# Sinkhorn's sums by products, the last pair's forms made at first use, and eight staging rows: one change to a three-layer kernel

## The chip, the core and the metric

The kernel runs on one core of a Trainium2 chip. The metric is the device time of one execution in microseconds (us). A core has five engines that run side by side and wait for one another by semaphores: TensorE (PE), VectorE (DVE), ScalarE (ACT), GpSimd (POOL) and SyncE (SP), which here issues all transfers; each works through its instructions in one fixed order.

## The reference

Linear attention on 4 x 8 heads, then a dense layer pair, then eight experts on 2304 tokens, each expert weighted by a gate that is normalised by rows and columns eight times:

```python
logits = x @ w_gate                       # 2304 x 8
P = np.exp(logits - logits.max())
for _ in range(8):
    P /= P.sum(1, keepdims=True) + 1e-09
    P /= P.sum(0, keepdims=True) + 1e-09
    P *= N / E
for e in range(E):                        # w1[e]: 512 x 1024, w2[e]: 1024 x 512
    out += P[:, e:e + 1] * (np.maximum(x @ w1[e], 0.0) @ w2[e])
```

## The kernel before

The first 650 us hold the attention part and the dense layers. The change concerns the experts after them. Their work is a list `order` of 48 positions (p, q): eight experts in two halves of their hidden width are p, and q counts three pairs of token blocks (2 x 384 tokens each). A position n has a layer 1 and a layer 2. Each is a 2x2 block product with seven products instead of eight (Winograd's scheme); the seven stand in `SLOTS` as p1, p5, p6, p3, p7, p2, p4. A product (L828) is twelve instructions of 128x384, since every operand is split into a high and a low part and three of the four part products are kept.

The left operands are "forms" of the weights (`split_forms`, seven for each layer, made on POOL, ACT and DVE), the right operands forms of the tokens: b11, t1, t2, b22, t3, b21, t4, where b are the blocks and t their differences. `split_form` makes one: a cast on ACT (L604) and a subtraction on DVE (L605). The token forms of a pair are made once, stored to DRAM as `xv`, and loaded for each expert half into one of four buffers `xvv` (768 KB a form, L700), the next one when a slot's product has freed a buffer. Pairs 0 and 1 are made during the last dense layer; for pair 2, `forms(NPR - 1, ...)` makes them beside layer 1 of position 0 (differences on POOL, L629) and sums the gate logits with twenty 128x384 products (L636) and transposes (L648).

Layer 1 leaves four hidden blocks r; `hidden_forms` makes their seven forms (differences on POOL, L852). In the main loop layer 2 of position n and layer 1 of position n + 1 alternate slot by slot, and `tick()` takes one step of a side task each time: first `sinkhorn`, then `gate_first`, which multiplies the accumulated first expert by its gate (L965), at the end `finish_pair`, which transposes (L977), copies (L978) and stores rows. Experts from the second on have the gate multiplied into their hidden blocks (L892), and so need the gate table `prT` in DRAM.

`sinkhorn` sums columns over partitions by an all-reduce on POOL, nine times. The program is reordered by a scheduler, so that the code's order and the engines' orders differ.

Of the kernel before, what the change touches and what calls it, by code (L numbers as in the profile page):

```python
# [20 lines left out]
def tile_features_attention__moe__sinkhorn_moe(  # L21
# [578 lines left out]
    xv = dram.tile([NPR, NS, P, 2 * KH * NB], F32, name="xv")  # L600
    prT = dram.tile([NE, (NTT + 3) // 4 * 4 * P], F32, name="prT")
# [5 lines left out]
    def forms(q, temp, part_, pg, turned, eng):  # L607

        t0 = 2 * NB * q

        def b(k, j):
            return accT[:, KH * (k - 1) : KH * k, t0 + (j - 1) * NB : t0 + j * NB]


        uses = {"b21": [(0, 1)], "t1": [(1, 0)], "b11": [(0, 0), (1, 0)], "b22": [(1, 1)]}
        done = [0, 0]
        of = {}
        for nm in ("b21", "t1", "b11", "b22", "t2", "t4", "t3"):
            if nm[0] == "b":
                src = b(int(nm[1]), int(nm[2]))  # L620
            else:
# [7 lines left out]
                eng.tensor_sub(src, lhs, rhs)  # L629
            v = part_()  # L630
            split_form(src, v)
            nc.sync.dma_start(xv[q, FORMS.index(nm)], v.bitcast(F32).rearrange("p a k n -> p (a k n)"))
            for blk, k in uses.get(nm, ()):
# [8 lines left out]
        for blk in range(2):  # L642
            gs = temp("gs").rearrange("p k n -> p (k n)")[: 2 * NE, :NB]
            nc.scalar.copy(gs, pg[blk][: 2 * NE, :NB])
            pt = turned()
# [3 lines left out]
            i0 = t0 // P + blk * nt  # L649
            nc.scalar.copy(lt[:, i0 : i0 + nt], pt[:, :nt])  # L650
            yield

    def early_forms(q, pool):
        return forms(
            q,
            lambda nm: pool.tile([P, KH, NB], F32, tag="t", bufs=2, name=nm),
            lambda: pool.tile([P, 2, KH, NB], F32R, tag="v", bufs=3, name="xvs"),
            [psm.tile([P, 512], F32, tag="sm", name="psg") for _ in range(2)],
            lambda: psm.tile([P, 4, 2 * NE], F32, tag="sm", name="pt"),
            nc.vector,  # L660
        )
# [55 lines left out]
    for p in range(1, N1):  # L717
# [10 lines left out]
        for bi, (t0, n) in enumerate(blocks):  # L728
# [17 lines left out]
            if last and bi % 2 and bi < len(blocks) - 1:  # L746
                side.append(early_forms(bi // 2, xs))
# [24 lines left out]
    def allred(out, in_, op):  # L772
        nc.gpsimd.partition_all_reduce(out, in_, P, op)

    def sinkhorn():
        nc.vector.tensor_add(pr, lt[:, :, 0:NE], lt[:, :, NE : 2 * NE])
        mx = mb.tile([P, 1], F32, name="mx")
        nc.vector.tensor_reduce(mx, pr, AX.XY, ALU.max)
        mg = mb.tile([P, 1], F32, name="mg")
        allred(mg, mx, bass_isa.ReduceOp.max)  # L780
        yield
# [3 lines left out]
        for _ in range(8):  # L785
# [6 lines left out]
            nc.vector.tensor_reduce(cs, pr.rearrange("p t e -> p e t"), AX.X, ALU.add)  # L792
# [189 lines left out]
    def fetch_both(p):  # L982
        for _ in fetch(p):
            pass
# [90 lines left out]
```

## Time and profile before

| | |
|---|---|
| median of three runs | 2167.4 us (2164.7 to 2167.79) |
| the profiled execution, its own time | 2163.17 us |
| its span, first to last instruction | 2161.4 us |
| busy share PE / DVE / ACT / POOL | 96% / 80% / 40% / 36% |
| mean granted clock of PE | 0.981 |

Times in the rows count from the span's start. A line number such as L828 is that of the kernel before. Only where PE waits or runs at a lower granted clock can a change of the other engines' work gain anything.

### The profile page before, as it was taken

What the parts mean: (1) busy time and instruction counts of PE and PEld (TensorE: products, weight loads), DVE (VectorE), ACT (ScalarE), POOL (GpSimd) and SP (SyncE); (2) the same over time, 40 slices, a digit from 0 to 9 for tenths busy, and PEclk for the clock granted to TensorE, in tenths of its full rate; (3) what the DMA queues carried; (4) which work ended last, traced back from release to release, by engine and by line L of the source; (5) the groups of instructions that cost most, each with busy time, mean ns of one, the idle gap of its engine ahead of it and who ended that gap; (6) DMA issues with size and microseconds to landing.
All of it is one profiled execution on the core that took longest, in us unless ns stands there. A gap on an engine that the chain in (4) does not pass through costs nothing.

```text
span 2161.4 us, 31712 instructions
## 1 busy us (share of the span) xinstructions
PE 2070.0 (96%) x12326; PEld 1930.2 (89%) x12326; DVE 1725.5 (80%) x2167; ACT 872.9 (40%) x1508; POOL 780.0 (36%) x435
## 2 busy tenths in 40 slices
PE   8999999999996749999999999999999999999997
PEld 5566689888996749999999999999999999999997
DVE  5898657585666547999889888998898998988986
ACT  6786643222334315433334333333343333433432
POOL 3443200010005123545435445453354444534431
PEclk9999999999998879999999999999999999999998
DMA  4444241110247326566666666666766666667652
GB/s 117 108 105 116 78 127 57 39 59 1 112 161 287 122 74 240 209 232 210 235 237 225 222 243 223 225 213 228 241 224 223 231 231 229 217 224 244 205 197 96
DMA packets 156325, 381.91 MB, mean 177 GB/s; under 512 B 73616, under 2 KB 79888, under 8 KB 156176
## 3 DMA queue, kind: packets, MB, share of 16 engines
q1 hardware_dynamic: 156176, 379.88, 52.7%
q8 instruction: 99, 1.62, 0.3%
q14 instruction: 50, 0.41, 0.1%
HBM read 354.76 MB, written 24.93 MB: 176 GB/s over the span
## 4 chain that ended last, share of the span: by engine, by line
PE 84%; DVE 7%; DMA 4%; issue 3%; ACT 1%; POOL 1%; SPq 1%; DVEq 0%; POOLq 0%; ACTq 0%
PE psa L828 31%; PE psb L828 30%; PE ps L241 6%; PE ps L242 6%; PE ps L243 6%; DMA rb<-rden 2%; PE kvp L350 1%; PE psn L406 1%; DVE acc L965 1%; PE zp L357 1%; DMA rden<-comp 1%; DVE xl L605 1%; PE psd L415 1%; DVE acc L938 0%; DMA xl<-xv 0%
## 5 line engine op out<-in xcount | busy, mean ns | idle before, releaser
L828 PE MATMUL psb<-xl,xh 128*128 128x384 f32 x2400 | 447.3, 336 | 15.4 <-DVE mu L899 14.2
L828 PE MATMUL psa<-xl,xh 128*128 128x384 f32 x2400 | 449.0, 337 | 7.8 <-ACT xl L604 3.2
L828 PEld LDWEIGHTS psb<-xl,xh 128*128 128x128 f32 x2400 | 421.2, 189 | 16.5 <-DVE mu L899 14.6
L828 PEld LDWEIGHTS psa<-xl,xh 128*128 128x128 f32 x2400 | 422.3, 189 | 9.5 <-ACT xl L604 3.6
L852 POOL TENSOR_TENSOR t<-r,r 128x768 f32<-128x768 f32 x96 | 207.4, 2160 | 513.8 <-DVE r L892 462.2
L852 POOL TENSOR_TENSOR t<-r,t 128x768 f32<-128x768 f32 x96 | 233.8, 2435 | 17.3 <-issue 13.6
L828 PE MATMUL psa<-xl,w2v 128*128 128x384 f32 x960 | 182.8, 338 | 9.9 <-DVE xl L605 5.2
L828 PE MATMUL psb<-xl,w2v 128*128 128x384 f32 x960 | 181.7, 336 | 9.2 <-DVE xl L605 9.2
L938 DVE TENSOR_TENSOR acc<-psb,acc 128x768 f32<-128x768 f32 x163 | 154.9, 950 | 42.8 <-PE psb L828 39.0
L938 DVE TENSOR_TENSOR acc<-psa,acc 128x768 f32<-128x768 f32 x161 | 153.0, 950 | 40.9 <-PE psa L828 37.2
L605 DVE TENSOR_TENSOR xl<-t,xl 128x768 fp32r<-128x768 f32 x131 | 179.9, 1373 | 5.8 <-ACT xl L604 5.7
L828 PEld LDWEIGHTS psa<-xl,w2v 128*128 128x128 f32 x960 | 170.3, 191 | 11.0 <-DVE xl L605 5.6
L828 PEld LDWEIGHTS psb<-xl,w2v 128*128 128x128 f32 x960 | 169.0, 189 | 9.5 <-DVE xl L605 9.5
L604 ACT CAST xl<-t 128x768 fp32r<-128x768 f32 x131 | 109.6, 837 | 115.4 <-POOL t L852 48.4
L390 POOL PARTITION_ALL_REDUCE eq<-eq x64 | 90.9, 1466 | 136.8 <-ACT eq L389 136.8
L241 PE MATMUL ps<-xh,w0h 128*128 128x288 f32 (+3 forms) x384 | 130.9, 341 | 3.3 <-ACT r L262 3.1
L605 DVE TENSOR_TENSOR xl<-r,xl 128x768 fp32r<-128x768 f32 x96 | 130.1, 1356 | 1.7 <-ACT xl L604 0.5
L242 PE MATMUL ps<-xl,w0h 128*128 128x288 f32 (+3 forms) x384 | 129.6, 338 | 0.0
L243 PE MATMUL ps<-xh,w0l 128*128 128x288 f32 (+3 forms) x384 | 129.3, 338 | 0.0
L684 POOL TENSOR_TENSOR s<-wf 128x512 f32<-128x512 f32 x32 | 50.9, 1591 | 212.0 <-DVE xh L605 114.1
L242 PE MATMUL ps<-gl,w1h 128*128 128x288 f32 (+3 forms) x384 | 126.6, 336 | 0.0
L243 PE MATMUL ps<-gh,w1l 128*128 128x288 f32 (+3 forms) x384 | 126.2, 337 | 0.0
(199 smaller groups left out, 3761.1 us busy)
## 6 DMA issues: line engine op xcount, KB each, us to landing
xl<-xv SPq DMA_DIRECT2D x336, 768.0 KB
wf<-in_moe_w_dram SPq DMA_DIRECT2D x32, 1024.0 KB
gate<-prT SPq DMA_DIRECT2D x45, 384.0 KB
xv<-xvs SPq DMA_DIRECT2D x14, 768.0 KB
raw<-in_moe_w_in_dram SPq DMA_DIRECT2D x16, 512.0 KB
raw<-in_moe_w_out_dram SPq DMA_DIRECT2D x16, 512.0 KB
qnat<-in_q_dram SPq DMA_DIRECT2D x16, 288.0 KB
rb<-rden SPq DMA_DIRECT2D x32, 144.0 KB
```

Source lines behind the costliest of these rows:

```text
L241: nc.tensor.matmul(ps, ah, bh, start=first, stop=False)
L242: nc.tensor.matmul(ps, ah, bl, start=False, stop=False)
L243: nc.tensor.matmul(ps, al, bh, start=False, stop=last)
L350: nc.tensor.matmul(kvp[h * D : (h + 1) * D, : 2 * NF], t[:r, i, h], e, start=(i == 0), stop=(i == MT))
L357: ins = nc.tensor.matmul(zp[q0 : q0 + 32, : 2 * NF], ones[:r, :32], e, start=(i < 2), stop=(i >= MT - 1))
L390: nc.gpsimd.partition_all_reduce(eq[:, 1], eq[:, 0], P, bass_isa.ReduceOp.absmax)
L604: nc.scalar.copy(v[:, 0], src)
L605: nc.vector.tensor_sub(v[:, 1], src, v[:, 0].bitcast(F32))
L684: nc.gpsimd.tensor_tensor(s1, a(2, 1), a(2, 2), ALU.add)
L828: nc.tensor.matmul(ps[:, x, :NB], w[:, wi, k, cs], b[:, bi, k], start=first and k + i == 0, stop=k == KH - 1 and i == 2, skip_group_check= ...
L852: nc.gpsimd.tensor_tensor(t[nm], x, y, ALU.subtract)
L938: nc.vector.tensor_add(o, ps, o)
```

## The change

1. The column sums of `sinkhorn` are products of a matrix of ones with the sums per partition, into columns 384 to 511 of the PSUM tile that layer 1's chain a uses at that time (`spare`); the maximum goes to DRAM and comes back broadcast to all partitions. `sinkhorn` starts after position 1 instead of before position 0.
2. The forms of pair 2 are made when position 2 first needs them, straight into the buffers `xvv`, and stored from there for later use; the differences are on POOL as before. The logits of this pair are sixty products of 128x16, issued in layer 1 of position 2, into spare columns too.
3. The output rows go through two tiles allocated once, with eight row slots, instead of a new tile of two rows each time.
4. The two weight loads of a half are issued in two positions instead of one.

```diff
+    def last_form(i, x):
+        q = NPR - 1
+        def diff(nm, lhs, rhs):
+            if nm not in late:
+                late[nm] = hp.tile([P, KH, NB], F32, name="late" + nm)
+            nc.gpsimd.tensor_tensor(late[nm], lhs, rhs, ALU.subtract)
+            return late[nm]
...
+        split_form(src, x.rearrange("p (a k n) -> p a k n", a=2, k=KH))
+        nc.sync.dma_start(xv[q, i], x.bitcast(F32))
...
         while nxt[0] < min(n, NS * len(order)):
             m, i = divmod(nxt[0], NS)
-            nc.sync.dma_start(xvv[nxt[0] % XB].bitcast(F32), xv[order[m][1], i])
+            x = xvv[nxt[0] % XB]
+            if m == NPR - 1:
+                last_form(i, x)
+            else:
+                nc.sync.dma_start(x.bitcast(F32), xv[order[m][1], i])
             nxt[0] += 1
...
         nc.vector.tensor_reduce(mx, pr, AX.XY, ALU.max)
+        nc.sync.dma_start(mxd.rearrange("a p -> p a"), mx)
+        mr = hp.tile([P, 2, NB], F32, tag="gate", bufs=2, name="mr")[:, 0, :P]
+        nc.sync.dma_start(mr, mxd.to_broadcast([P, P]))
+        yield
+        yield
         mg = mb.tile([P, 1], F32, name="mg")
-        allred(mg, mx, bass_isa.ReduceOp.max)
-        yield
+        nc.vector.tensor_reduce(mg, mr, AX.X, ALU.max)
...
             nc.vector.tensor_reduce(cs, pr.rearrange("p t e -> p e t"), AX.X, ALU.add)
+            yield
+            ps = spare["tile"][:, 1, NB + it * NE : NB + (it + 1) * NE]
+            with tc.issue_after(spare["first"]):
+                nc.tensor.matmul(ps, ones, cs, start=False, stop=True, skip_group_check=True)
             cr = mb.tile([P, 1, NE], F32, tag="cr", name="cr")
-            allred(cr[:, 0], cs, bass_isa.ReduceOp.add)
-            yield
-            nc.vector.tensor_scalar(cr, cr, 1e-9, None, ALU.add)
+            nc.vector.tensor_scalar(cr[:, 0], ps, 1e-9, None, ALU.add)
...
+    def logits(nm, x):
+        nt = NB // P
+        o = spare["tile"][:, 0, NB : NB + 2 * nt * 2 * NE].rearrange("p (t e) -> p t e", e=2 * NE)
+        with tc.issue_after(spare["first"]):
+            for blk, k in USES.get(nm, ()):
+                n8 = 4 * KH + 2 * KH * blk
+                for kk in range(KH):
+                    for w, part in ((wg1, 0), (wg2, 1)):
+                        done[blk] += 1
+                        for t in range(nt):
+                            nc.tensor.matmul(
+                                o[:, blk * nt + t], x[:, part, kk, t * P : (t + 1) * P], w[:, KH * k + kk, : 2 * NE],
+                                start=False, stop=done[blk] == n8, skip_group_check=True,
+                            )
+        if nm == "b21":
+            i0 = 2 * NB * (NPR - 1) // P
+            nc.scalar.copy(lt[:, i0 : i0 + 2 * nt], o)
...
+    def finish_rows(t):
+        if not turned:
+            turned.extend(stage(NP, w) for w in range(2))
+        ps = bank("ab"[t // 2 % 2] + "1")
+        for h in range(2):
+            o = turned[t // 4 % 2][:, (t + h) % 4]
...
     for i in range(NS):
         next(l1)
-        next(last)
         next(w2n)
...
-    side.append(sinkhorn())
...
+        if n + 1 == NPR - 1:
+            side.append(sinkhorn())
```

The order of POOL's instructions, from the start of position 0's hidden forms. `mg` and `cr` are all-reduced, `t` are differences of hidden blocks, `s` and `wf` belong to the weight forms, `late` to the last pair's forms; an ISA row without operands is an instruction that the all-reduce brings with it. Before:

```order
L773 ISA
L773 ISA mg<-mx 128x1 [waits DVE_49]
L852 ISA
L852 TENSOR_TENSOR t_7279<-r_7185,r_7234 128x768 [waits Activation_49,Pool_49]
L852 TENSOR_TENSOR t_7283<-r_7211,t_7279 128x768 [waits PE_49,Pool_49]
L852 TENSOR_TENSOR t_7287<-r_7211,r_7185 128x768
L773 ISA
L773 ISA cr<-cs 128x8 [waits DVE_49]
L852 ISA
L852 TENSOR_TENSOR t_7329<-r_7256,t_7283 128x768 [waits Activation_49,Pool_49]
```

After:

```order
L683 TENSOR_TENSOR s<-wf_5_7227 128x512 [waits DMAHW5_49,DVE_49,Pool_49]
L689 TENSOR_TENSOR s<-wf_4_6214,s 128x512 [waits DVE_49]
L685 TENSOR_TENSOR wf_5_7227<-wf_5_7227 128x2x256 [waits Pool_49]
L684 TENSOR_TENSOR s<-s,wf_5_7227 128x512 [waits DVE_49]
L894 TENSOR_TENSOR t_7215<-r_7157,r_7194 128x768 [waits Activation_49]
L894 TENSOR_TENSOR t_7219<-r_7176,t_7215 128x768 [waits Pool_49]
L894 TENSOR_TENSOR t_7223<-r_7176,r_7157 128x768
L894 TENSOR_TENSOR t_7263<-r_7211,t_7219 128x768 [waits Activation_49,Pool_49]
L715 TENSOR_TENSOR latex<-acc,latex 128x768 [waits DVE_49] x2
```

The all-reduces and the instructions that come with them are gone, and the last pair's differences have moved in between the hidden ones.

The order of PE's instructions at the end of position 3 and the start of position 4, the same place by the number of products ahead of it (psa and psb with a number are single PSUM tiles). Before:

```order
L828 MATMUL psa_8164<-xl_88,w2v3_7081 128x384 [waits DVE_49,Activation_49]
L828 MATMUL psa_8164<-xl_88,w2v3_7081 128x384 x11
L828 MATMUL psa_8146<-xl_88,xh_87 128x384 [waits DMAHW0_49,DVE_49]
L828 MATMUL psa_8146<-xl_88,xh_87 128x384 x11
L828 MATMUL psb_8163<-xl_88,w2v4_7082 128x384 [waits DVE_49,Activation_49]
L828 MATMUL psb_8163<-xl_88,w2v4_7082 128x384 x11
L828 MATMUL psb_8371<-xl_88,xh_87 128x384 [waits DMAHW1_49,DVE_49]
L828 MATMUL psb_8371<-xl_88,xh_87 128x384 x11
```

After:

```order
L832 MATMUL psa_8065<-cs_8179,ones_98 128x8 [waits DVE_49,Activation_49]
L867 MATMUL psb_8066<-xl_88,xh_87 128x384 [waits DMAHW0_49,DVE_49]
L867 MATMUL psb_8066<-xl_88,xh_87 128x384 x11
L867 MATMUL psa_8065<-xl_88,xh_87 128x384 [waits DMAHW7_49,DVE_49]
L867 MATMUL psa_8065<-xl_88,xh_87 128x384 x11
L867 MATMUL psb_8338<-xl_88,xh_87 128x384 [waits DMAHW1_49,DVE_49]
L867 MATMUL psb_8338<-xl_88,xh_87 128x384 x11
L832 MATMUL psa_8065<-cs_8252,ones_98 128x8 [waits DVE_49]
L867 MATMUL psa_8065<-xl_88,xh_87 128x384 [waits DMAHW2_49,DVE_49]
L867 MATMUL psa_8065<-xl_88,xh_87 128x384 x11
```

The ones products (L832) wait for DVE's column sums in the middle of PE's queue, and the layer-1 product after the second one writes to the same tile and waits for DVE; layer 2's products have moved away from here.

The order of SP's transfers where the gate table `prT` is stored. Before:

```order
L812 DMA prT<-tp 40x1x32 [waits DMAHW6_49]
L812 DMA prT<-tp 40x1x32 [waits DMAHW7_49]
L812 DMA prT<-tp 40x1x32 [waits DMAHW0_49]
L700 DMA xl<-xv 128x1536 [waits DMAHW1_49,PE_49]
L812 DMA prT<-tp 40x1x32 [waits DMAHW2_49]
L812 DMA prT<-tp 40x1x32 [waits DMAHW3_49]
```

After:

```order
L703 DMA xl<-xv 128x1536 [waits DMAHW1_49,PE_49]
L850 DMA prT<-tp 40x1x32 [waits DVE_49]
L850 DMA prT<-tp 40x1x32 x2
L850 DMA prT<-tp 40x1x32 [waits DMAHW0_49]
L850 DMA prT<-tp 40x1x32
L850 DMA prT<-tp 40x1x32 [waits DMAHW2_49]
```

Form loads stood between the stores at three places; now the stores stand together, and the next form load comes after the last of them.

## Rows read from the trace of the kernel before

**Rows 1.** The page: PE's busy share and its granted clock in 40 slices.
```profile
PE   8999999999996749999999999999999999999997
...
PEclk9999999999998879999999999999999999999998
```

**Rows 2.** Windows by stage: length, busy PE, PEld, DVE, ACT, POOL, clock, DMA share, GB/s.
```profile
657.50:682.00 24.50, 21.56 (x111) 19.99 (x111) 22.03 (x17) 13.13 (x22) 20.17 (x11) 0.93 0.83 302
682.00:743.80 61.80, 36.68 (x168) 34.87 (x169) 24.87 (x65) 14.94 (x20) 10.16 (x10) 0.75 0.42 151
743.80:808.40 64.60, 36.68 (x169) 35.23 (x169) 24.65 (x43) 17.18 (x25) 16.82 (x13) 0.76 0.27 90
808.40:866.70 58.30, 58.30 (x339) 58.30 (x338) 45.44 (x39) 30.95 (x42) 25.52 (x13) 1.00 0.67 236
866.70:958.70 92.00, 88.44 (x506) 87.17 (x505) 89.81 (x86) 35.43 (x48) 40.84 (x21) 1.00 0.63 220
1016.90:1046.10 29.20, 29.20 (x171) 29.20 (x170) 24.62 (x25) 8.81 (x11) 9.09 (x5) 1.00 0.67 241
```

**Rows 3.** Chain of waits, 600 to 900 us: start, length, what it was.
```profile
671.73 10.08 DMA xl<-xv
...
700.69 5.80 issue
706.49 0.44 POOL cr L773
...
835.64 4.16 PE psa L828 x24
```

**Rows 4.** POOL groups, 650 to 810 us: busy, mean ns, idle before, what ended it.
```profile
L852 POOL TENSOR_TENSOR t<-r,r 128x768 f32<-128x768 f32 x5 | 9.9, 1973 | 21.4 <-issue 16.4 <-ACT r L896 5.0
L852 POOL TENSOR_TENSOR t<-r,t 128x768 f32<-128x768 f32 x5 | 9.8, 1950 | 13.8 <-issue 13.6
...
L773 POOL PARTITION_ALL_REDUCE cr<-cs x8 | 3.9, 486 | 44.8 <-issue 31.2 <-DVE cs L792 13.5
```

**Rows 5.** DVE groups, 650 to 960 us, the same columns.
```profile
L605 DVE TENSOR_TENSOR xl<-t,xl 128x768 fp32r<-128x768 f32 x22 | 30.9, 1404 | 5.8 <-ACT xl L604 5.7
...
L792 DVE TENSOR_REDUCE cs<-pr 128x8 f32<-128x144 f32 x8 | 3.4, 425 | 0.2
...
L790 DVE TENSOR_TENSOR pr<-pr,rs 128x144 f32<-128x144 f32 x8 | 2.4, 305 | 0.2
...
L796 DVE TENSOR_SCALAR cr<-cr 128x8 f32<-128x8 f32 x8 | 1.4, 170 | 58.5 <-POOL cr L773 58.5
```

**Rows 6.** Timeline of DVE, 800 to 960 us: start, length, instruction and count.
```profile
838.27 2.60 DVE L605 TENSOR_TENSOR hv<-t,hv 128x768 fp32r<-128x768 f32 x1
...
865.14 5.11 DVE L965 TENSOR_TENSOR acc<-acc,gate 128x768 f32<-128x768 f32 x2
...
935.91 3.55 DVE L965 TENSOR_TENSOR acc<-acc,gate 128x768 f32<-128x768 f32 x4
```

**Rows 7.** Chain of waits: small products on PE, at three places.
```profile
607.49 0.29 PE pt L648 x3
...
659.92 0.70 PE psa L636 x4
...
2126.21 0.44 PE psb L977 x4
```

**Rows 8.** Line L812, the gate table's stores: ns on SP, minimum, median, maximum.
```profile
L812 SPq DMA_DIRECT2D prT<-tp x16: 653/653/800, 791.0 to 802.7; - x16
```

**Rows 9.** The page: the chain's shares of the span by line.
```profile
PE psa L828 31%; PE psb L828 30%; PE ps L241 6%; PE ps L242 6%; PE ps L243 6%; DMA rb<-rden 2%; PE kvp L350 1%; PE psn L406 1%; DVE acc L965 1%; PE zp L357 1%; DMA rden<-comp 1%; DVE xl L605 1%; PE psd L415 1%; DVE acc L938 0%; DMA xl<-xv 0%
```

**Rows 10.** Chain of waits at the end.
```profile
2143.61 2.02 DMA out_dram<-wf
...
2147.80 2.01 DMA out_dram<-wf
...
2152.51 3.19 DMA out_dram<-wf
```

More of the change, by code (lines that the diff above doesn't have):

```diff
@@ L648, in forms @@
                 nc.tensor.transpose(pt[:, i], gs[:, i * P : (i + 1) * P], ident[: 2 * NE, : 2 * NE])
-            i0 = t0 // P + blk * nt
+            i0 = 2 * NB * q // P + blk * nt
             nc.scalar.copy(lt[:, i0 : i0 + nt], pt[:, :nt])
             yield
[L653 to L661, printed above, removed]
     xhv = xh.rearrange("p k n -> p (k n)")
@@ L770, in sum_tile @@
         return hp.tile([P, KH, NB], F32, tag="t", bufs=4, name=nm)
[L772 to L773 removed]
+    spare = {}
     def sinkhorn():
@@ L784, in sinkhorn @@
         yield
-        for _ in range(8):
+        for it in range(8):
             rs = mb.tile([P, NTT, 1], F32, tag="rs", name="rs")
@@ L905, in layer1 @@
             x = xvv[(NS * n + i) % XB].rearrange("p (a k n) -> p a k n", a=2, k=KH)
-            product(ps, w1v[i], x, nm in ("p1", "p5", "p2"))
+            ins = product(ps, w1v[i], x, nm in ("p1", "p5", "p2"))
+            if i == 0:
+                spare.update(tile=a, first=ins)
+            if n == NPR - 1:
+                logits(FORMS[i], x)
             load_forms(NS * n + i + 1 + XB)
@@ L966, in gate_first @@
             yield
+    turned = []
+    def finish_rows(t):
[4 more added lines that the diff above has]
+            o = turned[t // 4 % 2][:, (t + h) % 4]
+            for c in range(KD):
+                nc.tensor.transpose(ps[:, h, c * P : (c + 1) * P], accT[:, c, (t + h) * P : (t + h + 1) * P], ident)
+            (nc.scalar.copy if h else nc.vector.tensor_copy)(o, ps[:, h])
+            nc.sync.dma_start(out[(t + h) * P : (t + h + 1) * P, :], o)
     def finish_pair(q):
@@ L971, in finish_pair @@
         for i in range(0, n2, 2):
-            ps = bank("ab"[i // 2 % 2] + "1")
-            o = stage(NP + q * n2 + i, i // 2 % 2)
-            for h in range(2):
-                t = q * n2 + i + h
-                for c in range(KD):
-                    nc.tensor.transpose(ps[:, h, c * P : (c + 1) * P], accT[:, c, t * P : (t + 1) * P], ident)
-                (nc.scalar.copy if h else nc.vector.tensor_copy)(o[:, h], ps[:, h])
-                nc.sync.dma_start(out[t * P : (t + 1) * P, :], o[:, h])
-            yield
-    def fetch_both(p):
-        for _ in fetch(p):
-            pass
-    last = forms(
-        NPR - 1, sum_tile, form_tile, [bank("a2").rearrange("p a n -> p (a n)")[:, i * 512 : (i + 1) * 512] for i in range(2)],
-        lambda: bank("b2")[:, 0].rearrange("p (a n) -> p a n", n=2 * NE), nc.gpsimd,
-    )
+            finish_rows(q * n2 + i)
+            yield
     w2n = split_forms(N1, 1, w2v, sum_weights)
@@ L993, in tile_features_attention__moe__sinkhorn_moe @@
         next(l1)
-        next(last)
         next(w2n)
-    for _ in last:
-        pass
-    for _ in w2n:
-        pass
-    side.append(sinkhorn())
+    for x in (l1, w2n):
+        for _ in x:
+            pass
     made = hidden_forms(0)
@@ L1015, in tile_features_attention__moe__sinkhorn_moe @@
         if q == 1 and p + 1 < NP:
-            fetch_both(p + 1)
+            weights = fetch(p + 1)
+            next(weights)
+        elif q == NPR - 1:
+            next(weights, None)
         w1n = split_forms(p + 1, 0, w1v, sum_weights) if q == NPR - 1 and p + 1 < NP else iter(())
```

49 lines of the change are left out of this document (37 added, 12 removed).

## Prediction

> **What bounds the kernel now.** I read the page first. TensorE (PE) is busy 96% of the span; what is lost lies mostly in two places, a dip of its busy share and granted clock in slices 13 to 15 of 40, and the last slice [rows 1]. Then I cut the expert phase into stages by counting its products: layer 1 of the first position is 84 of them, and each position n after that is 168 (its layer 2 and the layer 1 of position n + 1). Undisturbed, a block of 24 takes 4.16 us [rows 3], 0.1733 us each, so the floors are 14.6 us and 29.1 us, and the steady window shows 29.2 [rows 2]. The first three stages took 24.5, 61.8 and 64.6 us, with 36.7 us of PE time instead of 29.1 in the two long ones, since the granted clock there was 0.75 and 0.76 [rows 2]. So 9.9 + 32.7 + 35.5 = 78 us stand above the floor between 657 and 808 us. Positions 2 and 3 run at the floor; 4 to 6 take 92.0 us where 87.4 would do, and there VectorE (DVE) is busy 89.8 of 92.0 us: DVE sets the pace [rows 2].
>
> The chain of waits says what the 78 us are. It goes through GpSimd (POOL): an all-reduce of 0.44 us, in front of it some 6 us of "issue" in which POOL waits for nothing that the profile shows, then four small DVE instructions, then a form, then PE [rows 3]. The POOL groups add these gaps up: 31.2 us ahead of eight sums and 30 us ahead of the differences that come after them [rows 4]; with three smaller groups of 6.6 to 7.6 us they are 82 us of the stretch. POOL's order shows an extra instruction at each change between all-reduce and difference, and the gaps stand there. The other early wait is 10.08 us for a form's load at 671.73 [rows 3], when the DMA engines were 83% busy [rows 2].
>
> **The change, part by part.**
>
> *All-reduces to products.* The nine all-reduces leave POOL, and the switches with them. POOL then has only differences: its busy 10.2 and 16.8 us in positions 0 and 1 [rows 2] already hold most of them, and with four for the last pair at about 2 us (9.9 and 9.8 us for five [rows 4]), which stood ahead of them before, it needs under 40 of 58 us. Nothing else in these two stages comes near its floor: DVE was busy 24.9 and 24.7 us there [rows 2] with most of Sinkhorn's 18.6 us [rows 5] in it, which moves out; the last pair's forms move in with seven subtractions of 1.4 us [rows 5].
>
> *The last pair's forms.* Layer 1 of position 0 loses twenty 128x384 products (0.70 us for four [rows 7], 3.5 us), six transposes and seven stores from a stretch in which the DMA engines were full. Its floor is 14.6; I allow 3 us for the loads, which this stage wants every 2.1 us (768 KB, while 302 GB/s is what the stretch reached [rows 2]): 17.5 us, **-7**. Bounds: 14.6 (loads in time) and 22 (DVE held back by contended splits as now).
> Position 0: floor 29.1, plus 4 for the first hidden forms, which nothing covers (difference 1.95 us [rows 4], cast, subtraction 1.4 us [rows 5], before layer 2 can use it): 33, **-29**. Bounds 29.1 and 40 (the 10.08 us wait for a load comes back).
> Position 1 gets the logits: 60 products of 128x16, each with a 128x128 weight load. No row has that shape. The nearest is a 128x128 transpose, 0.44 us for four [rows 7], 0.11 each; below, a 16x16 transpose at 0.10 (0.29 for three [rows 7]). I take 0.1, since both rows are near: 6 us, on PE's own path. 29.1 + 6 = 35.1: **-29.5**. Bounds 32 and 42.
>
> *Sinkhorn now runs in positions 2 to 4*, and the gate multiplications in 5 and 6. Its nine DVE groups of eight were 18.6 us busy, from 3.4 us down to 1.4 us [rows 5]; with logit sum, maximum, padding and transpose 20 us. DVE was busy 45.4 + 89.8 = 135.2 us in positions 2 to 6 [rows 2], so it now needs 155 us against floors of 145.6 and against the 150.3 us that these positions took. Only if it filled every gap would this cost 5 us more than before.
> Contention changes this number. A subtraction of 128x768 takes 2.60 us in one place, two gate multiplications take 5.11 us in another, and four take 3.55 us elsewhere, 0.89 each [rows 6]: a factor of up to 2.9, with POOL busy in the long cases. Two of the nine Sinkhorn steps multiply two arrays in SBUF (about 2.4 us each of the 18.6 [rows 5]); they ran while POOL sat in its gaps. Stretched by half of that factor they add 4 to 5 us.
> The Trainium skill (SBUF — State Buffer, "Who interferes with whom") says that a DVE instruction with two SBUF inputs shares a read port with GpSimd and that the one blocks the other, while reductions on this chip never contend. The trace agrees for the long and short subtractions; by that rule only the two multiplications stretch (at most 4.9 x 1.9 = 9 us), and without it the sum would be 4 to 5 us smaller.
> Two more waits lie there. The sixteen stores of the gate table occupy SP for 0.65 to 0.80 us each [rows 8], 11 us in a row; before, three form loads stood between them, now all sixteen stand together ahead of the next load, which must start three slots (12.5 us) before its use and takes several us to land. I put 3 us on it. And the maximum now goes to DRAM and back, with DVE's queue behind it (a form for layer 2 is next): store and broadcast load in the attention part are 1% and 2% of the span for 16 rounds [rows 9], 1.4 + 2.7 us, of which three instructions placed between cover about 3: 1 us. The eight 128x8 products have no row of their shape; from the 0.10 us of a 16x16 transpose to twice the 0.175 us of a 128x384 product [rows 7] they are 0.8 to 2.8 us, and I take 2.
> Together 5 + 4 + 3 + 1 + 2 = 15, less a third that overlaps, as PE waiting for a load or a sum lets DVE catch up: **+10** for positions 2 to 6. Bounds: 0 (the steps fall into DVE's idle 13 us of positions 2 and 3, and the gate multiplications into quiet stretches as the four at 935.91 did) and +25 (rival A).
>
> *Eight staging buffers.* At the end the chain holds three waits for an earlier store, 2.02 + 2.01 + 3.19 = 7.2 us [rows 10], because a row had to wait until its buffer's last store had landed. With eight row buffers a slot comes back only eight rows later. The last six rows now also alternate between two PSUM tiles. What remains: transposes, copies, and nine stores of 256 KB within some 8 us, which at the 302 GB/s of [rows 2] need 7.8 us themselves. I take **-8**; bounds -5 (stores queue) and -10.5.
> The weight loads, one per position instead of two at once, I cost at nothing: in the steady window the DMA engines are 67% busy and PE never waits [rows 2]; if that cover fails it costs one load's wait, some 4 us, in position 0.
>
> **Sum:** -7 - 29 - 29.5 + 10 - 8 = -63.5 us, against this execution's own 2163.2 us: 2099.7. The three timed runs have their median 4.2 us above the profiled one; between 2099.7 and 2104 I forecast **2101 us**. From position 7 on nothing changes, so the gain can't grow past about 90.
>
> **Rivals.**
> *A, the products couple PE and DVE.* Before, only POOL and DVE waited for Sinkhorn; now PE holds its queue until the column sums are there, and the next product of that chain stands until DVE has read the result. In the changed order a layer-1 product waits for DVE right behind the ones product. One contended DVE instruction ahead of each is 2.6 us [rows 6]: 8 x 2.6 = 21 us, plus the loads: +25 in place of +10, 2116. For it: DVE has no slack in positions 4 to 6 [rows 2]. Against: most column sums stand several DVE instructions ahead of PE's product. By the Trainium skill (PSUM — Partial Sum Buffer, "PSUM bank collisions raise a hardware error") no engine may read a bank while PE writes into it, at other columns either; the added waits in the order are what that asks for, and no run yet shows their price.
> *B, the start stays slow.* The loads and the first forms, not POOL, held position 0: the 10.08 us wait [rows 3] returns in each of the three first stages at half its size, and the clock stays down: +16, 2117. Against: the stores that filled the queues have gone to later positions.
> *C, DVE takes it all in.* Positions 2 to 6 cost nothing more and the end gives 10: 2089.
> *D, slower.* Each of the eight iterations again costs PE what it costs now: 78 us less the start's 10, over eight, is 8.5 us an iteration, one pair of slots (2 x 4.16 us). This would be so if PE's product always stood a full pair of slots behind a DVE queue that itself waits for PE; above 8 us an iteration the 63.5 us are gone, at 8.5 it ends at 2167 or above. Against: the DVE part of an iteration is 18.6 / 8 = 2.3 us [rows 5], a quarter of a pair of slots. That the all-reduces' gaps don't vanish can't be, as no all-reduce is left in the stretch.
>
> **How the numbers follow.** Forecast 0.70 (2084 to 2112), A 0.11, B 0.09, C 0.06, D 0.04. For 8 in 10 the range takes in A, B and most of C: 2083 to 2120. 0.2% (4.3 us) is about what a measurement here can tell from no change; only D ends slower, and within 0.2% lies a sliver of D and B: faster 0.95, same 0.01, slower 0.04.
>
> **What would show it.** No POOL gap of 6 us between 657 and 810 us; the first three stages at 16 to 19, 31 to 36 and 33 to 37 us with a granted clock near 1; 60 logit products at about 0.1 us; position 4 or 5 the longest of the later ones, with DVE busy all of it; no wait for an output store at the end, and under 12 us from the last product to the end. I am wrong if PE's waits in positions 2 to 5 come to more than 25 us, or if the form loads still end the waits in positions 0 and 1.

## The result, and the profile after

| | before | after |
|---|---|---|
| median of four runs each | 2166.7 us | 2116.4 us (2113.3 to 2118.0) |
| ratio, 95% interval | | 0.977 (0.975 to 0.978) |
| span of the profiled execution | 2161.4 us | 2115.2 us |

The change gains 50 us. 2101 us were forecast, so 15 us of the gain are missing: 2116.4 us lies inside the range of 2083 to 2120 us, but above the 2084 to 2112 us of the forecast itself, and at the 2116 and 2117 us of rivals A and B. Where the 15 us are shows in the stages. The page of the changed kernel, PE's busy share and granted clock in 40 slices, answers to [rows 1]:

```profile
PE   8999999999999989899999999999999999999998
...
PEclk9999999999999999999999999999999999999999
```

The deep dip has gone; in the expert part two slices (15 and 17, from 740 and from 846 us on) stay at 8. The windows by stage (layer 1 of position 0, then positions 0 to 6; columns as in [rows 2]) are cut at the same counts of products:

```profile
660.80:678.10 17.30, 15.40 (x86) 14.45 (x85) 12.97 (x12) 8.76 (x13) 15.11 (x10) 1.00 0.78 270
678.10:707.30 29.20, 29.20 (x169) 29.03 (x169) 22.85 (x18) 17.87 (x23) 14.76 (x7) 1.00 0.62 238
707.30:743.20 35.90, 35.90 (x231) 35.90 (x230) 28.81 (x26) 21.61 (x30) 19.75 (x11) 1.00 0.43 155
743.20:780.90 37.70, 32.09 (x171) 31.77 (x170) 23.61 (x34) 17.81 (x26) 12.63 (x8) 0.91 0.51 176
780.90:812.70 31.80, 30.75 (x178) 29.93 (x176) 25.93 (x48) 9.54 (x12) 4.25 (x3) 1.00 0.54 191
812.70:849.50 36.80, 32.16 (x175) 31.84 (x176) 33.30 (x50) 16.22 (x23) 16.98 (x10) 0.91 0.48 165
849.50:887.80 38.30, 31.32 (x169) 30.42 (x167) 30.99 (x35) 11.97 (x17) 12.51 (x7) 0.96 0.60 221
887.80:921.10 33.30, 31.35 (x168) 30.71 (x169) 33.29 (x33) 10.21 (x13) 12.05 (x6) 0.95 0.72 243
```

The first three stages take 17.3, 29.2 and 35.9 us at full clock (forecast 17.5, 33 and 35.1). Positions 2 to 6 take 178 us, against 58.3 + 92.0 = 150.3 in [rows 2]: +27.7, where the sum had +10. PE stands idle for 20.2 us of these five stages (before: 3.6) and is busy for 157.7 us (before: 146.7), with a granted clock of 0.91 to 0.96 in four of them: a wait costs more here than its own length. DVE's busy time is 147 us of 178, less than the 155 that the prediction gave it, so over the five stages DVE is not full. But in position 6 it is (33.29 of 33.3 us), and in position 4 nearly (33.30 of 36.8 us).

From 657 to 810 us POOL's groups hold no all-reduce. Of "issue" they have one gap of 9.9 us, ahead of the difference at 753.87 us, in the stall of position 2 that is shown next (columns as in [rows 4]):

```profile
L894 POOL TENSOR_TENSOR t<-r,t 128x768 f32<-128x768 f32 x8 | 18.1, 2259 | 10.2 <-issue 9.9
L894 POOL TENSOR_TENSOR t<-r,r 128x768 f32<-128x768 f32 x8 | 18.1, 2259 | 14.9 <-ACT r L959 14.9
```

The chain in position 2 (700 to 790 us) shows the maximum's trip, and the logits and a product of the ones ahead of and behind it, which answer to [rows 7]:

```profile
709.58 2.58 PE psa L932 x24
...
740.06 6.72 DMA mxd<-mx
...
746.80 4.77 DMA mr<-mxd
...
753.79 4.21 PE psa L867 x12
...
774.96 0.12 PE psb L832 x2
```

Store and load take 11.5 us instead of 4.1. DVE stands still for 6.8 us behind the reduction that waits for them, ACT's exponential (L819) waits for DVE, the ReLU behind it (L959) waits too, and PE for that, 5.6 us. ACT's timeline, and PE's waits in this stage:

```profile
752.10 0.42 ACT L819 ACTIVATE pr<-pr,mg 128x144 f32<-128x144 f32 x1 [9.29 <-DVE mg L818]
...
752.93 0.80 ACT L959 ACTIVATE r<-psa 128x768 f32<-128x768 f32 x1
...
PE psa L867 <- ACT r L959: 5.6, 1, 5.6
```

PE's next twelve products take 4.21 us, twice the time of a product in [rows 3]. The granted clock from 753.8 to 758.0 us is 0.50, the lower of its two levels (1.2 against 2.4 GHz).

DVE's groups from 738 to 860 us (columns as in [rows 5]):

```profile
L826 DVE TENSOR_TENSOR pr<-pr,rs 128x144 f32<-128x144 f32 x8 | 6.8, 845 | 0.2
L837 DVE TENSOR_TENSOR pr<-pr,cr 128x144 f32<-128x144 f32 x8 | 4.0, 499 | 0.2
L836 DVE TENSOR_SCALAR cr<-cr 128x8 f32<-128x8 f32 x8 | 3.8, 481 | 0.2
...
L828 DVE TENSOR_REDUCE cs<-pr 128x8 f32<-128x144 f32 x8 | 3.4, 427 | 0.2
L824 DVE TENSOR_SCALAR rs<-rs 128x18 f32<-128x18 f32 x8 | 3.4, 426 | 0.1
L823 DVE TENSOR_REDUCE rs<-pr 128x18 f32<-128x144 f32 x8 | 2.4, 300 | 0.2
L825 DVE RECIPROCAL rs<-rs 128x18 f32<-128x18 f32 x8 | 2.1, 258 | 0.1
```

With L834 and L835 (1.3 and 1.6 us) the nine groups are 28.8 us instead of 18.6. Reductions and reciprocals keep their length; multiplications and two small scalar steps stretch. In position 4 stretched steps stand in PE's way, as its chain (700 to 925 us) shows; POOL makes four differences from 812.95 to 821.5 us:

```profile
813.15 1.85 DVE pr L837
...
815.25 2.01 DVE xh L606
817.26 1.69 DVE rs L824
818.95 0.87 DVE xl L606
...
819.87 6.22 PE psa L867 x23
```

Elsewhere in this trace the first three take 0.31, 0.68 and 0.17 us. PE waits 4.6 us for the last subtraction, and its next 23 products take 2.2 us longer than at the rate of [rows 3].

The chain in position 5 (700 to 925 us) holds the gate table: sixteen stores from 854.88 on, then

```profile
865.84 1.80 DMA prT<-tp
...
867.78 6.77 DMA gate<-prT
...
874.57 3.56 DVE acc L1032 x4
...
891.24 8.40 DVE acc L1032 x4
```

All twelve gate multiplications now stand between 874.6 and 911.8 us; before, from 865.1 to 939.5 [rows 6]. From 874.6 to 900.5 us the chain runs through DVE alone, with these multiplications (three of them at 2.6 us instead of 0.95) among its other work. The end of the chain (2080 to 2116 us) has no wait for a store any more, against three in [rows 10]:

```profile
2102.62 2.12 PE psb L867 x12
...
2105.69 0.59 ACT wf L1046
...
2106.33 0.67 PE psa L1045 x4
```

### The profile page after: what moved, and what is told of

It is laid out like the page before. It is cut to its first block, busy times and chain, and to the rows that moved or that the text cites. A ratio compares the mean times of both kernels' runs of the same rounds, so it can differ in the third digit from the quotient of the medians.

```text
span 2115.2 us, 31745 instructions
## 1 busy us (share of the span) xinstructions
PE 2067.2 (98%) x12376; PEld 1930.2 (91%) x12376; DVE 1730.3 (82%) x2168; ACT 872.5 (41%) x1505; POOL 772.9 (37%) x426
## 4 chain that ended last, share of the span: by engine, by line
PE 88%; DVE 6%; DMA 3%; ACT 1%; SPq 1%; issue 1%; POOL 0%; DVEq 0%; ACTq 0%
PE psb L867 32%; PE psa L867 32%; PE ps L241 6%; PE ps L242 6%; PE ps L243 6%; PE kvp L350 1%; PE psn L406 1%; DMA rb<-rden 1%; PE zp L357 1%; PE psd L415 1%; DVE acc L1032 1%; SPq L850 0%; PE psq L386 0%; DVE w2v L606 0%; DVE eq L391 0%
## 5 line engine op out<-in xcount | busy, mean ns | idle before, releaser
L867 PEld LDWEIGHTS psa<-xl,xh 128*128 128x128 f32 x2400 | 422.4, 190 | 17.5 <-DVE xl L606 7.5
L1005 DVE TENSOR_TENSOR acc<-psb,acc 128x768 f32<-128x768 f32 x163 | 155.0, 951 | 40.1 <-PE psb L867 36.3
L1005 DVE TENSOR_TENSOR acc<-psa,acc 128x768 f32<-128x768 f32 x161 | 153.0, 950 | 41.9 <-PE psa L867 38.3
L606 DVE TENSOR_TENSOR xl<-t,xl 128x768 fp32r<-128x768 f32 x128 | 185.3, 1448 | 1.6 <-ACT xl L605 1.4
L605 ACT CAST xl<-r 128x768 fp32r<-128x768 f32 x96 | 80.3, 837 | 161.7 <-PE psa L867 83.3
```

The lines of the kernel that those rows point to most:

```text
L605: nc.scalar.copy(v[:, 0], src)
L606: nc.vector.tensor_sub(v[:, 1], src, v[:, 0].bitcast(F32))
L867: ins = nc.tensor.matmul(ps[:, x, :NB], w[:, wi, k, cs], b[:, bi, k], start=first and k + i == 0, stop=k == KH - 1 and i == 2, skip_group_ ...
L1005: nc.vector.tensor_add(o, ps, o)
```

## The experiments

The unchanged work ahead of the experts ended between 657 and 665 us in the profiled executions of these kernels, and this goes into every total. So each run is read first by its stages. Length of the stages in us, cut at the same counts of products:

| run | total | layer 1 + pos. 0 + 1 | 2 | 3 | 4 | 5 | 6 | sum |
|---|---|---|---|---|---|---|---|---|
| before | 2166.7 | 150.9 | 29.1 | 29.1 | 30.0 | 31.1 | 30.9 | 301.2 |
| after | 2116.4 | 82.4 | 37.8 | 31.8 | 36.8 | 38.4 | 33.3 | 260.4 |
| all-reduces at the new place | 2158.4 | 84.0 | 67.2 | 53.7 | 34.4 | 33.8 | 29.6 | 302.6 |
| before, sums by products alone | 2122.8 | 99.5 | 34.9 | 30.5 | 30.0 | 31.1 | 30.9 | 256.9 |
| own maximum | 2108.4 | 82.4 | 29.4 | 31.8 | 37.6 | 36.6 | 35.0 | 252.7 |
| one round of eight | 2098.9 | 84.0 | 37.7 | 29.4 | 29.7 | 31.2 | 30.9 | 242.9 |
| no products | 2107.2 | 82.4 | 37.5 | 33.3 | 37.2 | 30.6 | 30.9 | 251.9 |
| gate table on two queues | 2116.7 | 84.0 | 38.1 | 31.8 | 36.4 | 35.3 | 36.5 | 262.1 |
| no gate multiplications | 2111.1 | 82.4 | 38.1 | 31.8 | 36.4 | 34.7 | 30.1 | 253.5 |
| two-row staging | 2124.6 | 84.0 | 37.4 | 31.8 | 36.3 | 37.6 | 33.4 | 260.5 |
| one slot a round | 2113.6 | 82.4 | 37.2 | 39.2 | 32.4 | 33.9 | 29.6 | 254.7 |
| one slot a round, own maximum | 2111.0 | 82.4 | 33.7 | 40.6 | 34.4 | 32.1 | 30.8 | 253.9 |
| own maximum, early | 2105.6 | 84.0 | 29.6 | 35.0 | 34.4 | 34.1 | 31.4 | 248.5 |
| old place, eight rows, own maximum | 2105.9 | 92.2 | 33.3 | 30.9 | 30.0 | 31.1 | 30.9 | 248.5 |

### What made the start slow

First the all-reduces at their new place, in positions 2 to 4:

```diff
-        nc.sync.dma_start(mxd.rearrange("a p -> p a"), mx)
...
-        nc.vector.tensor_reduce(mg, mr, AX.X, ALU.max)
+        nc.gpsimd.partition_all_reduce(mg, mx, P, bass_isa.ReduceOp.max)
...
-                nc.tensor.matmul(ps, ones, cs, start=False, stop=True, skip_group_check=True)
+            nc.gpsimd.partition_all_reduce(cr[:, 0], cs, P, bass_isa.ReduceOp.add)
```

> The changed kernel with maximum and sums as all-reduces on POOL again, at the new place (positions 2 to 4); the last pair's forms and the staging rows stay as changed. Theory 1, the idle time of POOL at each change between all-reduce and difference made the start slow: the gaps of some 6 us come back, now in positions 2 to 4, and these three become 20 to 25 us each longer than their floor of 29.1, so the total is 2140 to 2175 us; positions 0 and 1 stay at 29 and 36 us. Rival, the old loads, forms and stores of the last pair held the start (rival B of the prediction), and the gaps only filled waiting time: positions 2 to 4 stay within 10 us of those of the changed kernel and the total is 2105 to 2127 us.

Ratio to before 0.996 (0.9945 to 0.9974). The POOL groups of this run from 742 to 865 us have the old gaps at the new place:

```profile
L889 POOL TENSOR_TENSOR t<-r,t 128x768 f32<-128x768 f32 x5 | 10.1, 2028 | 15.4 <-issue 15.2
L827 POOL PARTITION_ALL_REDUCE cr<-cs x8 | 4.2, 520 | 47.0 <-issue 28.8 <-DVE cs L825 12.3 <-ACT my L876 5.9
```

Against the changed kernel positions 2 and 3 grow by 29.4 and 21.9 us, and positions 0 and 1 stay short. This is theory 1 in the total and the gaps; the rival (2105 to 2127), rival B of the prediction, falls. The sizes by stage are off: 20 to 25 us over the floor were expected for each, and positions 2, 3 and 4 stand 38.1, 24.6 and 5.3 us over it.

Then the kernel before with one part of the change, the sums:

```diff
-            allred(cr[:, 0], cs, bass_isa.ReduceOp.add)
...
+            ps = spare["tile"][:, 1, NB + it * NE : NB + (it + 1) * NE]
+            with tc.issue_after(spare["first"]):
+                nc.tensor.matmul(ps, ones, cs, start=False, stop=True, skip_group_check=True)
```

> The kernel before (2166.7 us) with one part of the change: the eight column sums are products into spare PSUM columns; the maximum stays an all-reduce, Sinkhorn and the last pair's forms stay where they were (position 0 on, forms stored and loaded), two-row staging stays. Theory 1, the changes between all-reduce and difference on POOL were the stall: positions 0 and 1 fall from 61.9 and 64.6 us to 32 to 40 us each, less one pair of gaps of some 15 us for the maximum; total 2110 to 2130 us. Rival, the form loads (10.08 us in the chain) and the forms themselves hold the start: positions 0 and 1 stay over 50 us each and the total is 2145 us or more.

Ratio 0.979 (0.9775 to 0.981): this part alone gives 44 of the 50 us. Its windows of layer 1 and position 0:

```profile
662.70:688.20 25.50, 22.79 (x111) 21.08 (x111) 21.99 (x17) 12.96 (x22) 20.12 (x11) 0.87 0.84 311
688.20:730.90 42.70, 34.20 (x173) 32.73 (x174) 20.10 (x32) 15.51 (x21) 11.19 (x7) 0.84 0.53 198
```

Layer 1 stays at its old 25 us; position 0, with the one all-reduce that is left, is somewhat over the 40 that I allowed.

### The maximum's trip through DRAM

```diff
-        nc.sync.dma_start(mxd.rearrange("a p -> p a"), mx)
-        mr = hp.tile([P, 2, NB], F32, tag="gate", bufs=2, name="mr")[:, 0, :P]
-        nc.sync.dma_start(mr, mxd.to_broadcast([P, P]))
...
-        nc.vector.tensor_reduce(mg, mr, AX.X, ALU.max)
-        nc.vector.tensor_scalar(mg, mg, -1.0, None, ALU.mult)
+        nc.vector.tensor_scalar(mg, mx, -1.0, None, ALU.mult)
```

> This is the changed kernel (2116.4 us) in which each partition subtracts its own rows' largest logit in place of the largest of all (the row sums that follow divide the shift out again); store, broadcast load and one reduction of the maximum go, the two empty slots behind them stay. Theory 1, the trip through DRAM with DVE's queue behind it is what made position 2 long: position 2 falls from 37.8 us to between 29 and 32 us with its granted clock at 1, and the total to 2107 to 2111 us. Rival, the wait only holds work that is late in any case (Sinkhorn's DVE load and its products): position 2 stays over 34 us, or what it gives back is lost in positions 3 and 4, and the total stays at 2114 to 2118 us.

Ratio 0.973 (0.971 to 0.974). Position 2 of this run is at the floor with a full clock, as theory 1 says:

```profile
741.80:771.10 29.30, 29.30 (x171) 29.30 (x170) 23.32 (x32) 18.60 (x27) 12.96 (x8) 1.00 0.62 225
```

So the trip costs 8.4 us of position 2. Positions 3 to 6 together take 0.7 us more than in the changed kernel.

### Sinkhorn's rounds and their products

```diff
         for it in range(8):
+            if it:
+                yield
+                yield
+                continue
```

> The changed kernel with one round of Sinkhorn's eight; in the slots of the other seven nothing is done, so seven rounds of normalisation are not computed. It prices what the rounds cost by DVE's time and their products. Theory 1, the rounds cost what the prediction put down for load and contention together, 5 + 4, and 2 for the products: positions 3 and 4 fall from 31.8 and 36.75 us to 29.1 and 30 to 31 us, position 2 keeps its wait for the maximum, and the total falls by 7 to 11 us before anything that the stores of the gate table give by standing elsewhere. Rival, the rounds fit into DVE's free time and positions 3 and 4 are long because of loads and POOL: they stay at 31 us or more and 35 us or more.

2098.9 us, ratio 0.968 (0.967 to 0.970). Positions 3 and 4 fall by 9.4 us (68.6 to 59.1), the size that theory 1 has, and below the rival's bounds of 31 and 35 us. The 9.4 us are a net figure, since five of the gate multiplications now stand in positions 3 and 4. And positions 5 and 6 fall too, by 9.6 us to what they were before the change, though only the last steps of the eighth round stood in them (849.7 to 853.5 us): their gate table comes earlier.

Without the products, with each partition's own sums:

```diff
-            ps = spare["tile"][:, 1, NB + it * NE : NB + (it + 1) * NE]
-            with tc.issue_after(spare["first"]):
-                nc.tensor.matmul(ps, ones, cs, start=False, stop=True, skip_group_check=True)
...
-            nc.vector.tensor_scalar(cr[:, 0], ps, 1e-9, None, ALU.add)
+            nc.vector.tensor_scalar(cr[:, 0], cs, 1e-9, None, ALU.add)
```

> The changed kernel in which the column sums are not summed over the partitions: the eight products with the ones are left out and DVE goes on with each partition's own column sums, so this part of the normalisation is not computed. It prices the coupling of PE and DVE by those products. Theory 1, the coupling is small here, as PE's waits on the reading of the sums come to 0.3 us in the changed kernel's chain: the total falls by 0 to 4 us, to 2112 to 2117 us. Rival A of the prediction, each product makes PE wait for DVE and the following product stand until the sum is read: the total falls by 10 to 20 us, to 2096 to 2107 us, and positions 3 and 4 (31.8 and 36.75 us) go to about 29 and 31 us.

Neither theory as I had put them. The total falls by 9.2 us, near A's bound, but positions 2 to 4, where the products stand, do not get shorter (106.3 to 108.0 us); positions 5 and 6 do, by 10.2 us. DVE's timeline of this run shows the transposition of the table's values at 803.71 (854.52 in the changed kernel), so that the wait for its rows now falls into position 4:

```profile
803.71 0.33 DVE L842 STREAM_TRANSPOSE tp<-pad 128x160 f32<-128x160 f32 x1
...
824.52 0.96 DVE L1029 TENSOR_TENSOR acc<-acc,gate 128x768 f32<-128x768 f32 x1 [9.39 <-DMA gate<-prT]
```

Five gate multiplications stand in position 4 now, so positions 2 to 4 don't price the products by themselves. That these hardly hold PE up is read from the changed kernel's trace, where PE waits 0.3 us for the reading of the sums. What they do is tie each round to PE's slots: with them the transposition comes 51 us later. That the late end is what costs fits the run with one round; the runs under "When Sinkhorn ends" move it.

### The gate table in positions 5 and 6

```diff
-                nc.sync.dma_start(dst[b, t], tp[r0 : r0 + NE])
+                (nc.scalar if t % 2 else nc.sync).dma_start(dst[b, t], tp[r0 : r0 + NE])
...
         g = load_gate(0, q).rearrange("p a n -> p (a n)")
+        yield
```

> The changed kernel (2116.4 us) with two edits at the gate table: its sixteen stores go alternately to SP's and ACT's queue, and an empty slot lies between each gate load and the first multiplication with it. Theory 1, in position 5 PE waits because the stores stand on SP ahead of the form loads and because DVE's queue stands still for 6.5 us behind the multiplication that waits for the gate's rows: position 5 falls from 38.35 to 30 to 33 us and the total by 5 to 9 us, to 2107 to 2112 us. Rival, DVE is the bound there with its multiplications stretched by POOL, and the waits are only where it shows: positions 5 and 6 together stay over 68 us (now 71.65) and the total falls by less than 3 us.

The total stays, and the rival holds. SP was held 5.9 us instead of 11.6, no form load ends a wait of PE in positions 5 and 6 any more, and position 5 lost 3.0 us; but position 6 gained 3.2, and both together take 71.9 us. The edit isn't a clean removal of the stores' price: ACT's queue was held for 6.3 us by its eight stores, and the ReLU behind them came after 8.3 us of idle time. The stores began at the same time, 854.7, and the twelve multiplications stood even closer, from 871 to 902 us.

Without the gate multiplications:

```diff
-        g = load_gate(0, q).rearrange("p a n -> p (a n)")
         for c in range(KD):
-            o = accT[:, c, 2 * NB * q : 2 * NB * (q + 1)]
-            nc.vector.tensor_mul(o, o, g)
             yield
```

> The changed kernel without the twelve gate multiplications of the first expert's sums and the three loads of their rows, so expert 0's gate is not applied; Sinkhorn and the sixteen stores of the table stay where they are. It tells what positions 5 and 6 (38.35 and 33.3 us) pay for. Theory 1, they pay for the multiplications: the first waits 6.5 us for the gate's rows with DVE's queue behind it, and twelve within 37 us, eight of them stretched or close together, keep DVE full: position 5 falls to 30 to 33 us, position 6 to 29 to 30 us, the total by 8 to 12 us to 2104 to 2109 us. Rival, the sixteen stores ahead of the form loads on SP hold PE by themselves, as the prediction's 3 us for them say in small: position 5 stays at 35 us or more and the total falls by less than 6 us.

Position 5 is 34.7 us, between the two bounds, and position 6 30.1. The total fell by 5.3 us, less than theory 1 has and within the rival's 6; positions 5 and 6 of this execution lost 6.8. So of the 9.6 us the multiplications, with their wait, are 6.8. The other 2.8 us are a remainder that no run took away by itself. That the stores hold it is read from this run, where PE waits 3.6 us for form loads; its chain in position 5 has the last store, then the form load behind it, then PE.

```profile
870.00 0.65 SPq L850
...
870.76 4.36 DMA xl<-xv
...
875.26 4.49 PE psb L867 x16
```

### The end

```diff
-            o = turned[t // 4 % 2][:, (t + h) % 4]
+            o = stage(NP + q * n2 + i, i // 2 % 2)
...
+                nc.sync.dma_start(out[t * P : (t + 1) * P, :], o[:, h])
```

> The changed kernel with the two-row staging tiles of before at the end (the same transposes, copies and stores; two tiles in turn instead of eight row slots). Theory 1, the waits for an earlier store are what the end lost: the stretch from the last position's start to the end goes from 29.1 back to 37 to 38 us, the total rises by 7 to 10.5 us to 2123 to 2127 us, and nothing else moves. Rival, the end is set by PE, copies and the 256 KB stores themselves, and what was gained there came from PE running into the end at a full clock: the total rises by less than 4 us.

Total +8.2 us; from the last position's start (2088.3) to the end of the span (2125.0) it is 36.7 us instead of 29.1, and the sum of the stages is the same. The chain has its three waits again, 6.0 us, as theory 1 says:

```profile
2108.24 2.00 DMA out_dram<-wf
...
2112.41 2.03 DMA out_dram<-wf
...
2117.07 2.00 DMA out_dram<-wf
```

### When Sinkhorn ends

```diff
             nc.vector.tensor_mul(pr, pr, cr.to_broadcast([P, NTT, NE]))
-            yield
+        yield
```

> The changed kernel (2116.4 us) with the same computation, but each of Sinkhorn's eight rounds takes one slot of the program's order instead of two (the second empty slot of a round goes). So Sinkhorn ends in position 3 instead of position 5, and the twelve gate multiplications can spread over positions 4 to 6 as before. Theory 1, positions 4 to 6 are long because Sinkhorn ends late: its rounds run there beside differences on POOL, and three pairs' gate multiplications are pressed into 37 us (before: 73 us): positions 4, 5 and 6 fall from 36.75, 38.35 and 33.3 us to about 30, 31 and 31 us, position 3 rises by up to 6 us, and the total is 2100 to 2109 us. Rival, DVE's demand in positions 2 to 6 is the bound wherever it stands: what 4 to 6 lose, 2 and 3 take, and the total is 2113 to 2119 us.

Both are half right. Positions 4 to 6 fall by 12.5 us (108.4 to 95.9), the multiplications spread over 843 to 899 us; position 3 rises by 7.4. Its chain shows why: a round on DVE (here from the reading of one sum, L834, to the next column sums, L828) with layer-1 additions (L962) before and behind it, for which PE's layer-1 product waits; and, later, a product of the ones that waits for such an addition:

```profile
811.51 0.96 DVE mu L962
812.47 0.08 DVE cr L834
...
814.56 0.43 DVE cs L828
814.99 0.90 DVE ma L962
...
815.93 2.35 PE psb L867 x12
...
820.41 0.97 DVE my L962
...
821.42 0.40 PE psa L832 x2
```

PE stands idle for 6.2 us of position 3, in many waits of at most 1.1 us. The products of the ones have 2.2 us of them, and 0.5 us stand behind these products, until the sum is read. This is rival A's mechanism at a small size; it appears when a round has one slot instead of two.

With the own maximum besides:

> As the run with one slot for a round, and each partition's own maximum instead of the trip through DRAM, with the two empty slots behind it gone too. Theory 1, the trip (8 us in its own run) and the late end of Sinkhorn add up: position 2 at 29 to 33 us, positions 4 to 6 at 30 to 31 us each, total 2093 to 2101 us, below the run that leaves the forms and Sinkhorn in their old places (2105.9 us). Rival, with Sinkhorn pressed into positions 2 and 3 beside the layer-1 additions DVE is full there: positions 2 and 3 together stay over 72 us and the total is 2104 us or more.

The rival holds: positions 2 and 3 take 74.3 us, and the total is 2111.0 us. The two gains don't add up.

With two slots a round, the own maximum, and without the two empty slots that the trip had:

```diff
-        yield
-        yield
         mg = mb.tile([P, 1], F32, name="mg")
```

> The changed kernel with each partition's own maximum and without the two empty slots behind it, but two slots for a round as changed: Sinkhorn ends in position 4, two slots earlier than in the first run with the own maximum (2108.4 us). Theory 1, an earlier end spreads the gate multiplications over more of positions 5 and 6: these fall from 36.6 and 35.0 us to 31 to 34 us each, position 4 stays at 35 to 38 us; total 2101 to 2106 us. Rival, the place of the end doesn't matter: 2107 to 2110 us.

2105.6 us, ratio 0.972 (0.970 to 0.973): the total and position 6 as theory 1 has them, with positions 4 and 5 at 34 us each. It beats both kernels, by 61 and 11 us.

### Was it worth moving the last pair's forms?

The kernel before with the sums as products (above), the new staging, and the own maximum:

```diff
-        allred(mg, mx, bass_isa.ReduceOp.max)
...
-        nc.vector.tensor_scalar(mg, mg, -1.0, None, ALU.mult)
+        nc.vector.tensor_scalar(mg, mx, -1.0, None, ALU.mult)
...
+            finish_rows(q * n2 + i)
```

> The kernel before with two parts of the change and one edit of mine: sums by products, eight staging rows, and each partition's own maximum in place of the maximum over all; the last pair's forms and Sinkhorn stay in positions 0 to 2. The run with the sums alone took 2122.8 us, with 42.7 us in position 0, where its chain holds the maximum's all-reduce with the idle time of POOL around it. Theory 1, that one trip to the all-reduce costs 8 to 12 us and the staging 8.7 us: 2101 to 2107 us, and then moving the last pair's forms brings nothing, since what it takes out of layer 1 and position 0 it puts back in positions 1 to 6. Rival, position 0 stays at 40 us or more because the form loads and stores hold it: 2111 to 2116 us.

2105.9 us, ratio 0.971 (0.969 to 0.973), theory 1, and the same as the run before it, with the same sum of stages (248.5). Moving the forms takes 8.2 us out of the first three stages (92.2 to 84.0; the logits' six are in that) and puts 8.2 us into positions 2 to 6 (156.3 to 164.5), where Sinkhorn starts two positions later. That its start is the reason was not tested apart, and the split of the weight loads differs between the two runs as well.

## Why the prediction was right, and where its size was off

The mechanism of the gain was right and its start well sized. That the total fell into the range is in part luck: the term for positions 2 to 6 missed its own upper bound, position 0 gave 3.6 us more than forecast, and the range reached up to 2120 us only because it took in rivals A and B.

- *All-reduces to products* (the largest part of -29 and -29.5): right. Put back, the gaps return with 51 us in two positions; the sums alone give 44 us. The Trainium skill (GPSIMD Engine Reference, "2.1 Instruction dispatch") gives the first call of a freshly loaded GpSimd routine some 6 us without an instruction in the profile; the 5.80 us of [rows 3] and the 5.7 us and more of the gaps in the run with the all-reduces are of that size. That each change between all-reduce and difference loads a routine anew fits the extra instruction in POOL's order, but no run shows it.
- *Layer 1, positions 0 and 1*: -7.1, -32.6 and -28.8 us against -7, -29 and -29.5. The 4 us for uncovered first forms in position 0 were not there; sixty logits took about 6.4 us (0.107 us each) against 6.
- *The end*: -8.6 against -8, and 7.6 by its own run.
- *Positions 2 to 6*: the term that was mis-sized, **+27.7 instead of +10**, and over its bound of 25. By its own parts:

| part | put | measured | by which run |
|---|---|---|---|
| DVE's demand, contention, products | 5 + 4 + 2 | 9.4 net, positions 3 and 4 | one round of eight |
| stores of the gate table ahead of form loads | 3 | 2.8, as a remainder | one round of eight, less the last row |
| the maximum's round trip | 1 | 8.4 | own maximum |
| "less a third that overlaps" | -5 | none seen | |
| late gate rows, multiplications pressed together | not in the sum | 6.8 | no gate multiplications |

Five steps failed. The trip's price was taken from a store and a load of other shapes in the attention part, 1.4 and 2.7 us; they took 6.72 and 4.77. What hangs behind a wait of DVE was named ("a form for layer 2 is next"), but not ACT's ReLU behind the exponential. The gate multiplications I had in positions 5 and 6 without asking what their lateness does. The discount had no row behind it: the parts, each from positions of its own, come to 27.4 us, nearly all of the 27.7. And no term held the lower clock after a wait: PE stood for 5.6 us in position 2, and without the trip the stage was 8.4 us shorter.

One reading of the stores was off: two form loads stood between them before (792.7 and 798.1 us), the third behind the last.

- *Contention*: of the Sinkhorn groups' 10.2 us, 6 are the two multiplications (10.8 against 4.8), where 4 to 5 were put; 4.4 are L824 and L836 (7.2 against 2.8), which I had taken as free of it; the others lost 0.2. I had read the page too narrowly: the Trainium skill (SBUF — State Buffer, "Who interferes with whom") names DVE's `tensor_scalar` among the operations that can contend for the shared ports. The trace agrees: L836, such an operation, took 156 to 1591 ns.
- *Rival A* had the right total (2116) with the wrong reason: in the changed kernel PE waits 0.3 us for the reading of the sums. With one slot a round its mechanism is seen, at 2.7 us in position 3.
- *Rival B* is out, by the first run above. *C* and *D* fail by the stages: +27.7, and 9.4 us for seven rounds, 1.3 us each.
- *The signs*: PE's idle time in positions 2 to 5 is 18.3 us, under the 25 us that would have made me wrong, and no form load ends a wait in positions 0 and 1. From the last product to the end it is 10.5 us, under 12. Three signs failed: position 0 is faster than the 31 to 36 us named, POOL has one gap of 9.9 us, and DVE is busy for 31.0 of the 38.3 us of position 5, the longest.

What stays open: with the own maximum and two slots positions 4 and 5 remain at 34 us. The trace of that run shows the waits of the changed kernel at a smaller size (in position 4 2.9 us for a subtraction, in position 5 2.9 us for a form load and 1.5 us for an addition), but no run took them away. Of the contention with POOL only its place in the trace was seen; no run took POOL's differences away. The weight loads (part 4 of the change) had no run of their own.

## What to carry to other kernels

A side task costs by where its end falls as well as by its own time: ask what waits for its result, and what gets pressed together when it is late. A wait on DVE of which the data come through DRAM is priced by the whole queue behind it, on ACT and PE too, and small transfers need a row of their own shape. When a large stall has one cause, try that edit alone: here the sums alone gave 44 of 50 us, and the harder part, moving the forms, nothing measurable (2105.6 against 2105.9 us, both with the own maximum). And price a wait of PE by the lower clock behind it too.

## What the runs showed of the hardware

- A store of 128 values of four bytes, one from each partition, took 6.72 us from issue to landing (6.90 in the run with one slot a round), more than the 4.77 us of the broadcast load of all of them to 128 partitions.
- A DVE scalar step on 128x18 elements took 0.17 us in the median of eight and 1.77 us at the longest, at 817.18 us, while POOL made differences from 812.95 to 821.5 us.
- A product of 128x8 in spare columns of a tile in use took 0.12 us in the chain for its two instructions, and PE waited 0.3 us in all for the reading of such columns.
- A wait of 5.6 us on PE was followed by products at half the rate: twelve in 4.21 us at a granted clock of 0.50. Without the trip behind this wait the stage was 8.4 us shorter.
